# Another order for the same operations in a hand-scheduled kernel of linear attention, Fourier mixing and MLP

## The chip, the cores and the metric

The kernel runs on one core of a Trainium2 chip. The time is the device time of one execution in microseconds (us). A profile shows one execution; its span, from the first instruction to the last, is a little shorter than that execution's device time.

## What is computed

The inputs are r, k, v (4 batches, 8 heads, 768 steps, 48 dimensions), a decay w and a bonus u per head and dimension, and two weights of an MLP. The attention is a linear recurrence over the steps:

```python
for t in range(S):
    cur = einsum('bhd,bhe->bhde', u * k[t], v[t])
    y[t] = einsum('bhd,bhde->bhe', r[t], state + cur)
    state = w * state + einsum('bhd,bhe->bhde', k[t], v[t])
```

Its output x, 768 x 384 in each batch, goes through a Fourier mix and an MLP:

```python
u = x + real(fft(fft(x, axis=1), axis=2))
un = (u - mean(u)) / sqrt(var(u) + 1e-6)
out = u + relu(un @ w_ch1) @ w_ch2
```

## The kernel before

The work is cut into 24 chunks i of 128 steps, six in each batch b. The Python functions do not issue instructions at once. Each `op(...)` records an operation with a name, an engine, a planner's duration and a function that issues it; some have an alternative (`other=`) on another engine or in another form. The 1241 operations are numbered as they are recorded. At the end `sch.emit(_order(sch))` issues them as the string ORDER (lines 92 to 129) lists them: `543` issues operation 543 in its first form, `523.1` in its alternative. As each engine runs its own instructions strictly in this order, ORDER sets for every engine what stands behind what; the order within one engine is all that counts, and between engines semaphores take care. ORDER lists 1192 of the 1241 entries; those left out are some of the 90 idle fillers.

The names used below, with the lines of kernel.py:

- k i, r i, v i: loads of chunk i on the queue of SP (lines 279 to 290). The tiles kr and vt have 4 buffers each.
- KR i (302): VectorE scales k and r by powers of the decay. V i (310/311): a cast of v, on ScalarE or VectorE.
- tp i (316) and KRT i (325/326): transposes of KR on TensorE and their copy out of PSUM; from chunk 15 on KRT i is a transposing DMA on the SP queue (319).
- PR i (327), VectorE. A i (337): scores on TensorE, into two PSUM tiles.
- AC i,a with MA i,a: the causal mask of either half a. Either ScalarE copies the scores (344) and GpSimd masks the copy (346), or VectorE does both at once (349) and AC is nothing.
- u i (369/372) and S i+1 (381/383): the state's update on TensorE, and its copy, on VectorE or ScalarE.
- de i (401/406), DE i (412), TT i (414/417), y i (426): the output of chunk i; X i (435) adds TT on VectorE. In the other form an identity matmul, xt i (432), adds TT in PSUM, and ScalarE only copies X i (438). The PSUM tile yd_ps has one buffer, so de of the next chunk waits until X is done.
- EO, HH, XF (489, 495, 503/508 for batches 1 to 3, 455/469 for batch 0): the folds of the Fourier mix on VectorE, along steps and along dimensions. EO b,0,. takes chunks 0, 1, 3, 4 of batch b, EO b,2,. chunks 2 and 5.
- fp b,g,n (546), TT2 (555/558), TR (565/569), mp (586), xr (597), UF (599/605), UB (608/612): both Fourier products, the residual, the centred rows; st, MV, sd, rstd (617 to 655): the variance. st on ScalarE is line 619.
- UNT b,sh (661): the transpose of UB for the MLP, in batch 0 on TensorE (630), later a DMA on the SP queue.
- hp hf,ft (678): three matmuls of the MLP's first layer, for half batch hf = 2b+sh and a block ft of 12; HT hf,ft (683 on ScalarE, 686 on VectorE) is its ReLU. mo hf,j,half (698): six matmuls of the second layer; osb (705) adds, and out (709) stores on the SP queue.
- W1, W2 (735): weights, loaded on the GpSimd queue, each gated by a small copy (734) on a chunk's KR or V.
- idle (203): a matmul on zeros that does nothing but keep TensorE busy.

Nearly all short-lived PSUM results (hp, mo, fp, mp, tq, idle) share the ring "mm" of three buffers, so the fourth hp in a row waits until the first one's HT is done.

The order as it stands interleaves: chunks of batch b+1 are attended while the MLP of batch b fills TensorE. At the start TensorE has only chunks and fillers; at the end only the MLP of batches 2 and 3.

The operations that the text names have these numbers: xt12 470, X12 471, de14 502, DE14 503, xt15 523, y15 522, X15 524, AC16,1 530, AC16,0 532, u16 534, X16 541, EO2,0,1 543, KR17 550, V17 551, X17 564, KR18 571, A18 575, u18 580, KR21 622, KR23 664, KRT19 590, r23 207, fp1,0,0 767, fp1,1,0 771, UB1,0 788, st1,4 816, hp2,0 1013, HT2,0 1014, HT2,6 1030, HT2,7 1032, HT2,10 1042, HT2,11 1044, out1,1 1036, v15 184, k17 188, V0 213, KRT0 215, MA15,0 516.

Of the kernel before, what the change touches and what calls it, by code (L numbers as in the profile page):

```python
# [89 lines left out]


ORDER = """
95 93 135 90 110 91 101 137 117 102 108 116 118 109 114 94 129 96 111 138 92 136 132 0 97 104 140 1 112 98 2 103 99 3 105 119 4 113 115 5 120 106 141
6 107 121 139 7 124 8 212 123 9 142 125 214 122 143 100 10 144 215.1 11 12 13 230 126 217 146 127 213 14 15 133 218 232 134 147 216 220 222 131 219
233.1 224 231 16 149 225.1 17 221 223.1 130 235 226.1 18 128 150 234 238.1 228 227 252 240 19 20 145 21 236 229 254 241.1 239.1 237 148 242 22 255
243.1 244.1 23 24 152 274 246.1 245 257 247.1 209 256 276 258.1 260 248 264 249 277 153 25 292 26 27 28 265 151 253 259.1 261 294 275 262 278 279 295
263 266 29 280.1 30 281.1 155 284 282 268 267 250 285.1 297 251 154 269 31 283 211 298.1 32 286 210 296 33 314 287.1 34 300 685 692 156 693 293 699
288.1 301 316 299.1 157 290 289 948 317 700 302 291 686 160 270 304 303.1 318 319 305.1 306.1 949 158 315 706 707 322.1 323.1 320 308.1 307 271 309.1
273 272 324 310 694 321 708 325.1 326.1 687 701 311 328.1 327 159 312 329.1 313 702 330 695 161 331 709 710 332 688 333 689 947 711 690 696 697 691
712.1 703 704 698 35 705.1 713.1 334 715 162 721 716 335 722.1 717 727 723.1 344 163 336 728 729 718 36 724.1 37 719.1 730.1 735 737 337.1 739 736.1  # L100
720.1 738.1 740 339 338 353 953 714 340.1 342 345 164 741 954 346 343 753 742 743 725.1 747 165 950 754 755 744 969 748 726.1 749 167 756 761 970
750.1 765 168 762 745.1 763 766 975 764 731.1 746.1 370 977 976 732.1 1007 347 733.1 978.1 348 751.1 372 1008.1 973 373 752.1 341.1 350 1005 371.1 349
166 974 352 955 1006 979 757.1 169 956.1 354 388 980 362 758.1 959 170 363.1 971 734 355.1 960 963 172 972 356 390 964 406 171 357 391 957 358.1 359.1
173 989 360 392 965 389 990.1 361 175 375 958.1 966 380 951 376.1 378 174 1003 381 759.1 377.1 981 379 1004 176 1001 351 982 398 432 407 178 364 1002
967 399.1 760 374 393 952 968 416 396.1 394.1 397.1 434 365 417.1 995 395.1 366 435 983 996.1 368 367 991 984 369 177 437 433 436 992 382 440.1 438.1
441.1 408 179 383 384 961 409.1 993 962 439.1 386 385 994 985 410 455 387 411 454 986 412 180 414 413 456 987 182 415 400 457 464 1033 473.1 183 472
401 465.1 1034 181 458 402 474 1035 185 459 490 404 403 462.1 1045 460 186 475 405 461 188 482 463.1 418 997 508 419 988 491 998 476 184 483 420 477
999 187 422.1 421 480 525 492 190 423.1 1009 478 424 1036 425 442 500 493 1046 426 193 427 443 509 1000 494 1010 1047 444 196 501 495 428 446.1 1048
445 431 498.1 1021 526 1011 481 447.1 510 430 496 466 448 517 467 449 1022 518.1 451 1012 450 527 429 534 452 767 453 768 771 1023 468 769 772 189 773
770 499.1 775 776 479 191 470 774 469 777 779 471 497 780 778 781 484 782 572.1 512 192 535 485 785 511 515.1 513 791 783 1024 786 797 784.1 787 514  # L110
792.1 798 799 194 793.1 486 806 516.1 807.1 788 195 488.1 794.1 487 800 529 550 489.1 812 805 530.1 532.1 589 818 813 571 819.1 808.1 519 520 197
820.1 809.1 580 38 814 198 521 821 789 39 810.1 523 522 815.1 40 524 822.1 826 811.1 588 502 823.1 581.1 1013 528 199 503 533.1 1017 504 552 1014 1037
790 1018.1 816.1 506 1019 801 1038 1025 817.1 795 573 1020 597 605 1039 1026 598.1 505 1049 796 802 607 507 1040 1065 1050 606.1 536 551 1066.1 1015
803 200 531.1 537 614 824.1 1063 1016 804 553 554 201 825 615 538 1027 555 1064.1 1043 1028 540 574 539 203 1044 1053 556 541 1079 1054 542 204 559
557 543 1061 560 1080 206 608 1067 1062 544 1077 1068 545 207 1073 1078 622 1029 1074 202 1075 1030.1 561 1051 1076 590 1041 639 563 1052 575 1042
1031 546 205 578.1 576 547 1055 208 1032.1 558 1057 1056 664 623 562 624 1069 577 564 566 1058 565 579.1 549 1093 567 1059 609 568 1060 591 1094 610
548 570 612 569 582 1070 666 611 1095 583 625 592 584 1071 1096 827 828 593.1 595 594.1 829 1072 613 839 586 840 830 841 835 596 836 842 585 831 640
832 587 833 837 1081 834.1 838 667 843 844.1 845 1082 846 847 848.1 849.1 851 1083 616 852 631 850.1 853 617 1084 857 618 866 641 854 858 859 878 867
620 619 868 879 626 860 872 880 869 865 1117 873 874 627 861.1 875.1 1118 881.1 629 862.1 621 628 886 855.1 1105 870 630 1119 856.1 863.1 632.1 633
871 642 1106 1120 864 634 882 635 876 1085 1107 637 636 1091 1086 638 1108 668 877 1092 883 599 671.1 669 672.1 1121 600 884 648 601 643 1122.1 649.1  # L120
1089 885 644.1 603 646 602 1101 604 665 647 1115 1090 1102.1 670 650 645.1 1116 1145 651 1103 652 1146.1 1087 1104 654 653 1113 1088 655 1097 1114 656
673 1098 657 1109 674 1099 675 1110.1 1111 1100 658 677 1135 1112 659 676 1141 1136 678 680 1142 679 681 682 1129 660 662 663 661 1130 684 683 1143
887 888 1131 889 1144 891 892 890.1 893 1132 899 900 894 901 895 896 902 897 903 1125 898.1 1127 1126 904 905 1128 911 906 907 912.1 917 913.1 1147
918 919 908 1151 1148.1 914 926 920.1 1139 1152 927 928 925 938 1140 932 929 939 940 1153 933 934 941 1154 930.1 935.1 946 942.1 931.1 1133 1155 943.1
1137 1134 1156 1123 909.1 1138.1 1157 1124.1 915.1 910.1 1171 1158 1169 916.1 1172 1183 1170 1173 936.1 1184.1 1193 1174.1 921.1 937.1 1211 1194 1217
922.1 944.1 1212 1221 945 1218.1 923.1 1205 924 1222 1187 1206 1149 1188 1185 1150 1175 1186 1207 1176 1209 1208 1197 1210 1223 1198 1195 1224 1165
1196 1166 1199 1167 1159 1200 1168 1219 1160 1163 1220 1189 1164 1190 1177 1191 1192 1233 1178 1181 1179 1234 1182.1 1180 1237 1235 1236 1161 1229
1162 1238 1230 1239 1240 1213 1231 1232 1225 1201 1202 1214 1203 1204 1226 1215 1216 1227 1228
"""


# [652 lines left out]
```

## Time and profile before

| | |
|---|---|
| median of 13 runs | 185.38 us (182.84 to 189.43) |
| profiled execution | 184.95 us, span 183.2 us, mean granted TensorE clock 0.991 |
| TensorE busy | 164.9 us (90%), of it 12.4 us matmuls on zeros |
| VectorE busy | 141.1 us (77%) |
| ScalarE busy | 117.3 us (64%) |
| GpSimd busy | 44.2 us (24%) |
| HBM | 20.03 MB read, 4.72 MB written |

In the profile PE is TensorE, PEld its weight loads, DVE VectorE, ACT ScalarE, POOL GpSimd and SP the engine whose queue issues most DMAs (SPq). L302 is line 302 of the kernel. Busy time is the sum of instructions; matmuls overlap, and their ends are modelled. A row such as "L686 DVE ... x22 | 11.8, 550" means 22 instructions, 11.8 us in all, 550 ns each.

### The profile page before, as it was taken

Reading aid. Unit: us, or ns where it says so; the run is one execution under the profiler, and the core shown is the slowest. Engines: PE = TensorE matmul, PEld = TensorE weight load, DVE = VectorE, ACT = ScalarE, POOL = GpSimd, SP = SyncE. Lnnn points to the kernel's source line nnn. Section 1 sums busy time; section 2 is a strip of 40 time slices with the busy share of each in tenths; the row PEclk is TensorE's granted clock in tenths of the full one; section 3 lists DMA queues with packets and bytes.
Section 4 is the critical chain, followed back from the end, with each engine's and each line's share of the span. In section 5 each row is a group of like instructions: output and inputs, shape, how many; then the busy total and the mean of one; then the engine's idle time right before and its main releaser. Section 6 shows DMA issues by size and latency. Waiting matters only on the chain.

```text
span 183.2 us, 4289 instructions
## 1 busy us (share of the span) xinstructions
PE 164.9 (90%) x1624; PEld 107.6 (59%) x1626; DVE 141.1 (77%) x322; ACT 117.3 (64%) x277; POOL 44.2 (24%) x67
## 2 busy tenths in 40 slices
PE   4799878999998999769799899999999999999991
PEld 1256557666565666467456466876666765566650
DVE  7799698998998699978999999899698753014322
ACT  2888882999896346438988635796742899840100
POOL 5024352031362453403213215043410000000000
PEclk9999999999999999988999999999999999999999
DMA  4999999999999799999799895175002070011223
GB/s 99 206 189 201 236 233 205 194 183 203 208 175 221 147 204 254 211 178 198 127 228 200 169 210 148 47 165 155 0 0 84 14 163 2 4 43 55 74 86 129
DMA packets 97828, 26.79 MB, mean 146 GB/s; under 512 B 92432, under 2 KB 97168, under 8 KB 97808
## 3 DMA queue, kind: packets, MB, share of 16 engines
q1 hardware_dynamic: 94480, 23.77, 61.7%
q0 software_dynamic: 2144, 2.36, 8.1%
q10 hardware_dynamic: 1184, 0.39, 1.0%
q8 instruction: 12, 0.20, 0.4%
q14 instruction: 8, 0.07, 0.2%
HBM read 20.03 MB, written 4.72 MB: 135 GB/s over the span
## 4 chain that ended last, share of the span: by engine, by line
PE 47%; DVE 29%; DMA 14%; issue 5%; SPq 2%; ACT 1%; DVEq 0%
PE mm L678 17%; PE mm L698 15%; DMA kr<-in_r_dram 8%; DVE KR L302 6%; PE mm L546 4%; PE mm L586 3%; DMA kr<-in_k_dram 3%; DMA UNT<-UB 2%; DVE X L435 2%; DVE PR L327 2%; DVE EO L489 2%; PE A_ps L337 2%; DVE HH L495 2%; DVE UF L599 2%; DVE MA L349 2%
## 5 line engine op out<-in xcount | busy, mean ns | idle before, releaser
L678 PE MATMUL mm<-UNT,W 128*128 128x384 bf16 x288 | 53.3, 326 | 1.3 <-DVE HT L686 0.9
L698 PE MATMUL mm<-W,HT 128*128 128x384 bf16 x288 | 50.7, 326 | 1.0 <-DMA W<-in_moe_w_ch_dram 1.0
L683 ACT ACTIVATE HT<-mm 128x384 bf16<-128x384 f32 x74 | 35.4, 490 | 16.8 <-PE mm L678 16.5
L698 PEld LDWEIGHTS <-HT 128*128 128x128 bf16 x288 | 27.1, 98 | 17.9 <-DMA W<-in_moe_w_ch_dram 1.4
L678 PEld LDWEIGHTS <-W 128*128 128x128 bf16 x288 | 26.4, 97 | 17.2 <-issue 1.8
L705 DVE SCALAR_TENSOR_TENSOR osb<-mm,rstd,UF 128x384 f32<-128x384 f32 x24 | 14.6, 611 | 22.4 <-PE mm L698 22.4
L346 POOL TENSOR_SCALAR_AFFINE_SELECT MA<-AC 128x512 bf16<-128x512 bf16 x27 | 19.1, 714 | 52.2 <-ACT AC L344 51.4
L414 POOL TENSOR_TENSOR TT<-V,DE 128x384 bf16<-128x384 bf16 x19 | 17.0, 897 | 33.6 <-ACT DE L412 27.8
L302 DVE TENSOR_TENSOR KR<-kr,wtab 128x768 bf16<-128x768 f32 x24 | 22.9, 956 | 2.1 <-DMA kr<-in_r_dram 1.7
L344 ACT CAST AC<-A_ps 128x512 bf16<-128x512 f32 x27 | 15.5, 585 | 8.9 <-PE A_ps L337 8.7
L546 PE MATMUL mm<-te_t,XF 128*128 128x193 bf16 x99 | 12.3, 257 | 3.2 <-DVE XF L503 2.1
L203 PE MATMUL mm<-zero 128*128 128x512 bf16 x39 | 12.4, 426 | 2.8 <-DVE zero L219 2.7
L349 DVE TENSOR_TENSOR MA<-A_ps,mtri 128x512 bf16<-128x512 f32 x21 | 14.2, 680 | 0.0
L686 DVE TENSOR_SCALAR HT<-mm 128x384 bf16<-128x384 f32 x22 | 11.8, 550 | 2.6 <-PE mm L678 2.5
L555 ACT CAST TT<-mm 97x386 bf16<-97x386 f32 x11 | 6.1, 597 | 11.7 <-PE mm L546 11.7
L310 ACT CAST V<-vt 128x384 bf16<-128x384 f32 x20 | 10.2, 512 | 4.7 <-DMA vt<-in_v_dram 3.2
L546 PEld LDWEIGHTS <-XF 128*128 128x128 bf16 x120 | 10.0, 101 | 5.0 <-DVE XF L503 2.2
L327 DVE TENSOR_TENSOR PR<-KRT 128x512 bf16<-128x512 bf16 x24 | 12.3, 514 | 0.1
L435 DVE TENSOR_TENSOR X<-yd_ps,TT 128x384 bf16<-128x384 f32 x18 | 9.9, 552 | 3.2 <-PE yd_ps L426 3.1
L325 ACT COPY KRT<-tp 128x1024 bf16<-128x1024 bf16 x10 | 10.1, 1014 | 2.6 <-PE tp L316 2.5
L599 DVE SCALAR_TENSOR_TENSOR UF<-mm,X 128x384 f32<-128x384 f32 x19 | 10.2, 556 | 1.8 <-PE mm L586 1.5
L619 ACT ACTIVATE lw<-UF,sm 128x384 f32<-128x384 f32 x18 | 11.0, 613 | 0.6 <-DVE UF L599 0.4
(90 smaller groups left out, 230.4 us busy)
## 6 DMA issues: line engine op xcount, KB each, us to landing
kr<-in_k_dram SPq DMA_DIRECT2D x24, 192.0 KB, 4.1
vt<-in_v_dram SPq DMA_DIRECT2D x24, 192.0 KB, 4.1
out_dram<-osb SPq DMA_DIRECT2D x24, 192.0 KB, 1.9
kr<-in_r_dram SPq DMA_DIRECT2D x23, 192.0 KB, 3.9
W<-in_moe_w_ch_dram POOLq DMA_DIRECT2D x6, 384.0 KB, 6.7
te_t<-te_c SPq DMA_DIRECT2D x1, 579.0 KB, 5.3
hid_t<-hid_c SPq DMA_DIRECT2D x1, 288.0 KB, 3.9
wrow<-in_w_dram ACTq DMA_DIRECT2D x1, 192.0 KB, 3.8
```

The costliest lines, as they stand in the source:

```text
L302: op(("KR", i), "DVE", 960, lambda: nc.vector.tensor_tensor(out=KR().rearrange("t s p (a d) -> t (s p) a d", a=2)[:, :, :, 0:D], in0=kr(). ...
L327: op(("PR", i), "DVE", 410, lambda: nc.vector.tensor_tensor(out=PR(), in0=KRT()[:, 0], in1=KRT()[:, 1], op=AluOp.mult), r=[("KRT", i)], w= ...
L344: op(("AC", i, a), "ACT", 590, lambda: nc.scalar.copy(AC(), A_ps[a]()), r=[("A", i)], w=[("AC", i, a)], new=[AC], use=[A_ps[a]], pri=pri, ...
L346: op(("MA", i, a), "POOL", 630, lambda: nc.gpsimd.affine_select(out=MA[a](), in_=AC(), pattern=[[0, NP], [1, 128]], base=0, channel_multip ...
L349: port=True, other=[("DVE", 680, False, lambda: nc.vector.tensor_tensor(out=MA[a](), in0=A_ps[a](), in1=mtri.unsqueeze(1).to_broadcast([12 ...
L414: op(("TT", i), "POOL", 830, lambda: nc.gpsimd.tensor_tensor(out=TT(), in0=V(), in1=DE().unsqueeze(2).to_broadcast([128, H, D]), op=AluOp. ...
L546: nc.tensor.matmul(fp()[:, par, :], lhsT=lhsT[:, g * CH:g * CH + 128], rhs=rhs, start=(nb == 0 and par == 0), stop=(nb == last and par == ...
L599: op(("UF", b, blk), "DVE", 650, lambda: nc.vector.scalar_tensor_tensor(out=parity(UF()[:, j, :]), in0=mp(), scalar=1.0, in1=parity(X()[:, ...
L678: nc.tensor.matmul(hp(), lhsT=W1[:, dt, ft * 128:(ft + 1) * 128], rhs=UNT()[:, :, dt, :], start=(dt == 0), stop=(dt == 2))
L683: op(("HT", hf, ft), "ACT", 495, lambda: nc.scalar.activation(out=HT()[:, ft, :], in_=hp(), func=Act.Relu, scale=-1.0), r=[("hp", hf, ft)] ...
L698: nc.tensor.matmul(mo(), lhsT=HT()[:, ft, j * 128:(j + 1) * 128], rhs=W2[:, ft, :], start=(ft == 0), stop=(ft == 11))
L705: op(("osb", hf, j), "DVE", 620, lambda: nc.vector.scalar_tensor_tensor(out=osb(), in0=mo(), scalar=rstd()[:, j:j + 1], in1=UF()[:, j, :], ...
```

## The change

Only the string ORDER differs. No operation, tile, wait or duration is edited. 1192 entries stand in either string. What changes is the place of many entries and the form of about 120. By kind, before and after: HT on ScalarE 74 and 81, on VectorE 22 and 15; masks on GpSimd 27 and 26, on VectorE 21 and 22; X on VectorE 18 and 16, on ScalarE 6 and 8, with as many xt matmuls (6 and 8); KRT on ScalarE 10 and 8, on VectorE 5 and 7; S on ScalarE 13 and 12, on VectorE 7 and 8. The number of idle fillers is the same.

The lines of ORDER that hold the operations named above, before (-) and after (+):

```diff
-95 93 135 90 110 91 101 137 117 102 108 116 118 109 114 94 129 96 111 138 92 136 132 0 97 104 140 1 112 98 2 103 99 3 105 119 4 113 115 5 120 106 141
-6 107 121 139 7 124 8 212 123 9 142 125 214 122 143 100 10 144 215.1 11 12 13 230 126 217 146 127 213 14 15 133 218 232 134 147 216 220 222 131 219
+118 93 135 90 108 114 110 91 137 101 117 109 95 116 111 94 102 92 98 138 136 105 0 97 129 1 107 140 96 2 112 3 132 99 113 104 4 119 5 106 120 141 6
+103 121 7 139 115 122 8 212 9 124 143 10 123 214 125 142 100 11 144 215 12 13 230 14 15 146 126 217 134 127 131 213.1 232 216 218 147 222 133 224 220
...
-401 465.1 1034 181 458 402 474 1035 185 459 490 404 403 462.1 1045 460 186 475 405 461 188 482 463.1 418 997 508 419 988 491 998 476 184 483 420 477
-999 187 422.1 421 480 525 492 190 423.1 1009 478 424 1036 425 442 500 493 1046 426 193 427 443 509 1000 494 1010 1047 444 196 501 495 428 446.1 1048
-445 431 498.1 1021 526 1011 481 447.1 510 430 496 466 448 517 467 449 1022 518.1 451 1012 450 527 429 534 452 767 453 768 771 1023 468 769 772 189 773
-770 499.1 775 776 479 191 470 774 469 777 779 471 497 780 778 781 484 782 572.1 512 192 535 485 785 511 515.1 513 791 783 1024 786 797 784.1 787 514
-792.1 798 799 194 793.1 486 806 516.1 807.1 788 195 488.1 794.1 487 800 529 550 489.1 812 805 530.1 532.1 589 818 813 571 819.1 808.1 519 520 197
-820.1 809.1 580 38 814 198 521 821 789 39 810.1 523 522 815.1 40 524 822.1 826 811.1 588 502 823.1 581.1 1013 528 199 503 533.1 1017 504 552 1014 1037
-790 1018.1 816.1 506 1019 801 1038 1025 817.1 795 573 1020 597 605 1039 1026 598.1 505 1049 796 802 607 507 1040 1065 1050 606.1 536 551 1066.1 1015
-803 200 531.1 537 614 824.1 1063 1016 804 553 554 201 825 615 538 1027 555 1064.1 1043 1028 540 574 539 203 1044 1053 556 541 1079 1054 542 204 559
-557 543 1061 560 1080 206 608 1067 1062 544 1077 1068 545 207 1073 1078 622 1029 1074 202 1075 1030.1 561 1051 1076 590 1041 639 563 1052 575 1042
-1031 546 205 578.1 576 547 1055 208 1032.1 558 1057 1056 664 623 562 624 1069 577 564 566 1058 565 579.1 549 1093 567 1059 609 568 1060 591 1094 610
+455 459 1035 402 474 185 460.1 462 997 473.1 404 475 458 186 403 998 463 405 1036 508 418 184 492 419 491 999 420 464 1045 188 461.1 465.1 476 988
+422.1 421 525 477 423.1 187 482 442 424 483.1 1009 425 1000 443 493 426 190 500 1046 427 478 193 480 428 1010 444 1047 510 431 446.1 445 501 1021 509
+479 1011 1048 447.1 526 196 494 517 449 466 495 448 467 430 1022 451 498.1 496 1012 450 518.1 429 527 453 771 452 767 768 1023 468 769 772 773 770
+499.1 534 189 775 497 470.1 774 469 191 776 572.1 777 471.1 779 783 780 778 781 511 484 192 782 512 481 535 485 785 513 486 515.1 516.1 194 791 784.1
+786 797 787 514 792.1 1024 488.1 798 799 487 793.1 529 788.1 806 800 195 794.1 807.1 818 489.1 550 819.1 808.1 805 519 812 571 820.1 37 813 520 810.1
+814 197 521 580 38 198 532 789 811.1 523.1 809.1 815 522 39 821.1 524.1 588 826 530 502 40 551 581 533 503 816.1 1013 801 199 1037 528 552 817.1 1014
+790 504 802 1017 795 1038 1015 822.1 1018.1 506 505 796 573 1039 589 531 823.1 507 1016 1019 605 1040 536 1020 1049 200 824.1 1065 803 1050 606.1 597
+607 825 804 1077 1066 598 537 1025 1078 1067 553 1026 201 538 1053 1068 614 554 1054 203 540 615 1027 555.1 557 556.1 539 1043 1028 574 204 1063 558
+1044.1 575 541 1064 206 1029 578 542 1061 576 590 608 559 543 1030 1041 560 1062 609 561 1042.1 207 1031 610 202 544 563 1079 1032 622 1073 1080 1055
+1074 205 545 1075 1056 546 1069 547 208 1076 639 562 624 1057 564 579 664 612 1070 623 565 592 611 1071 1051 548 1072 582 1058 566 1052 641 549 583
```

## The prediction

> **What bounds the kernel now.** I read first the slices of the page, to see which engine is full when (each digit is 4.58 us).
>
> ```profile
> PE   4799878999998999769799899999999999999991
> DVE  7799698998998699978999999899698753014322
> PEclk9999999999999999988999999999999999999999
> DMA  4999999999999799999799895175002070011223
> ```
>
> There are three stages. Up to about 65 us the DMA row is at 9: input chunks arrive no faster, and TensorE fills its waits with matmuls on zeros (39, 12.4 us in all). From 65 to 105 us VectorE is nearly full and TensorE has holes. From there to the end TensorE is at 9 without a break. The granted clock dips once, in the middle stage. The busy times by stretch (length, then PE, PEld, DVE, ACT, POOL, clock, DMA share, GB/s) size this:
>
> ```profile
> 72.00:78.00 6.00, 4.73 (x50) 2.74 (x47) 5.97 (x12) 2.53 (x7) 3.31 (x5) 1.00 1.19 223
> 78.00:84.00 6.00, 4.74 (x52) 4.04 (x53) 4.42 (x12) 2.77 (x6) 0.00 (x0) 0.74 0.99 196
> 84.00:90.00 6.00, 4.92 (x64) 3.64 (x63) 5.73 (x15) 5.64 (x17) 2.43 (x3) 0.98 0.74 141
> 90.00:96.00 6.00, 5.28 (x53) 3.41 (x53) 5.66 (x14) 5.27 (x16) 0.83 (x1) 1.00 1.08 213
> 96.00:102.00 6.00, 6.00 (x60) 3.77 (x58) 5.97 (x13) 5.24 (x15) 2.98 (x4) 1.00 1.05 201
> 102.00:108.00 6.00, 5.13 (x45) 2.95 (x43) 5.58 (x10) 3.40 (x8) 0.74 (x2) 1.00 0.89 173
> 150.00:160.00 10.00, 10.00 (x62) 5.93 (x61) 2.04 (x6) 9.46 (x24) 0.00 (x0) 1.00 0.08 25
> ```
>
> TensorE idles 1.27+1.26+1.08+0.72+0.87 = 5.2 us here. After 108 us it idles some 0.2 us up to its end at 179.5. So a wait removed in the middle stage shortens the run, and one that is added lengthens it. Which waits they are, the timeline of TensorE tells (start, duration; in brackets the idle time before and who ended it):
>
> ```profile
> 76.52 0.26 PE L546 MATMUL mm<-te_t,XF 128*128 128x193 bf16 x1
> 78.86 0.34 PE L546 MATMUL mm<-te_t,XF 128*128 128x193 bf16 x2 [2.09 <-DVE XF L503]
> 79.61 1.28 PE L546 MATMUL mm<-te_t,XF 128*128 128x193 bf16 x13 [0.40 <-DVE XF L508]
> ...
> 88.25 0.34 PE L369 MATMUL u_ps<-V,KR 128*128 128x96 bf16 x4 [0.48 <-DVE KR L302]
> 90.31 0.24 PE L401 MATMUL yd_ps<-UW,PR 128*128 128x2 bf16 x4 [0.87 <-DVE X L435]
> 104.37 0.65 PE L678 MATMUL mm<-UNT,W 128*128 128x384 bf16 x3 [0.87 <-DVE HT L686]
> ```
>
> The first pair is fp1, the Fourier matmuls of batch 1, behind the fold EO, HH, XF on VectorE. Then u18 waits for KR18. At 90.31 de14 waits for X15, as yd_ps has one buffer. At 104.37 an mlp1 matmul waits for HT2.6, which VectorE runs behind KR21 (102.90, 0.94 us). Right after the first pair the clock falls:
>
> ```profile
> 80.80:84.30 3.50, 3.50 (x40) 3.00 (x39) 2.09 (x6) 2.51 (x7) 0.12 (x1) 0.51 1.10 238
> ```
>
> **What the Trainium skill says.** "TensorE: Matmul & The Clock Gate", part 1 (The HAM clock gate), says that TensorE falls to half clock after an idle window of about 3.4 us and recovers after a busy one, and that the windows run free of the kernel. The trace agrees on rate and length (0.51 for 3.5 us), though TensorE was not wholly idle: 1.91 of 4.40 us busy from 76.4 to 80.8. "SBUF — State Buffer", section "SBUF: two separate sides", says that VectorE and GpSimd share a port pair as an exclusive lock, so that an operation of either blocks the other for its whole length. The trace agrees: the two wide HH of batch 1 took 2.11 us from 71.36 on, with a GpSimd TT (71.33) and a mask (72.11) beside them; those of batch 3, with GpSimd idle, 1.10. "Perfetto Trace Analysis", section "Tensor Engine Instruction", calls ACT, DVE and GPSIMD strict FIFO: what waits holds all behind it, as HT2.6 shows.
>
> **The change, part by part.** No operation is added except two identity matmuls (xt12, xt15), because X12 and X15 move from VectorE to ScalarE. All else is order and choice of engine.
>
> *Start to fp1.* KRT0 moves to ScalarE behind the six table exponentials (end 8.84): 8.84+1.01 = 9.85, against 8.45+0.69 = 9.14 before; V0 goes to VectorE. The chain then waits for chunk 5's load to 22.83 anyway, so I take 0. Without that cover it costs 0.7. On SP, v12 and v13 move behind r14, which lets KR13 and KR14 come earlier and V12, V13 later; out1.1 moves ahead of v15 and k17, whose data are wanted 17 us later. The bytes ahead of chunk 16 are the same, and KR16 started at 69.45, about 4 us (median landing 3.9) after its r was issued at 65.39. So EO1 begins at the same time: 0, within -0.5 to +0.7. The two weight loads that swap places on the POOL queue have the same bytes and gates: 0, inside the same bounds.
>
> *fp1.* The same operations stand between KR16 and the last XF, so the wait ends at the same time. u16 (0.28 us, 76.23 to 76.52) was done before the wait and now stands behind it: +0.28. xt12 is one more matmul there: +0.17 (start to start of the like one at 68.65). fp1.1.0 goes in front and takes two matmuls out: -0.17. Sum +0.28, at half clock up to +0.6; at least 0.
>
> *KR18 and u18.* VectorE does MA15.0 (0.68) before UF1.0, where it idled, and no longer between; UB1.0 (0.41) comes in. KR18 ends 0.27 earlier; I take -0.2 of u18's wait of 0.48, bounds -0.48 and 0.
>
> *X15 and HT2.0.* On ScalarE stand from about 88.0, UF1.5 being done: st1.3 0.80, AC16.0 0.59, UB1.4 0.61, X15 0.48, end 90.5. Before, X15 ended on VectorE at 89.71+0.55 = 90.26. Then AC16.1 0.59, V17 0.51, DE14 0.17, st1.4 0.80, HT2.0 0.49: end 93.0, against 91.49+0.49 = 92.0. The PSUM ring mm has three buffers, so the fourth mlp1 group waits for HT2.0. Counting on from 93.0 with 0.49 a group, y14 0.20 and de16 0.27, eight groups are done at 95.92 with u19 (0.17) still owed; before, eight and u19 at 95.86. So +0.23, taken as +0.3; bounds -0.3 (X15 runs before UB1.4's inputs matter) and +1.1 (one AC and V row, 0.59+0.51, more in front).
>
> *HT2.6 and HT2.7* go to ScalarE; VectorE gets HT2.11 and HT2.10 instead, behind X16 and EO2.0.1, none behind a KR. The wait of 0.87 goes: -0.87. Next late would be ScalarE: A18's two AC rows (1.17) stand before HT2.6, and counting as above each group finds its buffer with 0 to 0.2 us to spare. Bounds -0.87 and 0. On SP, KRT19 (1.3 us of issue) moves ahead of r23; KR23 now runs behind X17, which waited for y17 until 107.7, past r23's landing near 105.5+1.3: 0, uncovered +1.3.
>
> *From 105 us* TensorE is full with the same work; the last osb and its DMA (3.7 us after the last matmul) are the same. VectorE loses HTs there (22 to 15 over the run), which only adds slack: 0.
>
> Sum: 0+0.28-0.2+0.3-0.87 = -0.49. The profiled execution took 184.95 (span 183.2 and 1.75 around): 184.46. The median of the 13 runs is 0.43 above it: 185.38-0.49 = 184.89, say **184.9**.
>
> **Rivals.**
>
> *The clock stays up* (183.2). TensorE was busy for all 3.50 us at 0.51, so the dip cost at most 3.5x(1-0.51) = 1.7. If the two matmuls of fp1.1.0 within the wait, or the four scattered fillers before hp2.0 where three stood close together, keep a window busy enough, it goes: 184.9-1.7 = 183.2. For: spread of the runs, 182.84 to 189.43, shows that something that large comes and goes. Against: the wait itself stays.
>
> *ScalarE becomes the bound, slower.* Between the first TT2 of batch 1 and of batch 2 it gains two HT (0.98), two X (0.96), two AC (1.17) and loses two S (1.28) and a UB (0.61): +1.2 us, where from 84 to 102 it idles 0.36+0.73+0.76 = 1.85. If HT2.0 ends later than about 94, and HT2.6 behind A18's copies, each makes TensorE wait for a row of copies, 1.1 and 0.9: 184.9+2.0 = 186.9. For: strict order and three mm buffers. Against: the sum still fits.
>
> *Nothing gained, nothing lost*: the 0.87 comes back as the port lock, since two more masks (0.64 each) run on GpSimd in this stage beside VectorE's folds: 184.9+0.87, about 185.8. It lies within the forecast's own band.
>
> **How the numbers follow.** About 0.5% (0.9 us) is what a measurement of this kernel can tell from no change, so no change is 184.45 to 186.3. The forecast with the third rival (184.0 to 186.0) has 0.38: 0.08 under 184.45, 0.27 within, 0.03 above. The clock rival has 0.33, all faster but 0.02. The ScalarE rival has 0.29, slower but for 0.01. Faster 0.39, same 0.30, slower 0.31. The range leaves out a tenth at either side: 182.5 (clock rival less the -0.5 of the start, rounded) to 187.4 (ScalarE rival with the start's +0.5); the likeliest case's own range is 184.0 to 186.0.
>
> **What would show it.** HT before mlp1's first wait near 104 is no longer named, and TensorE is full from about 102; X15 ends near 90.5 and HT2.0 near 93.0, both on ScalarE; XF still ends a wait of about 2 us in fp1. It is wrong if fp1 starts more than 0.7 us earlier or later, if TensorE shows holes after 108 us, or if the clock row differs.

## The result

| comparison | kernel | median of it, us | median of the kernel before, us | ratio, 95% interval |
|---|---|---|---|---|
| first | changed | 183.70 (11 runs) | 185.70 | 0.9905 [0.9866, 0.9943] |
| second, chip 1 | changed | 180.81 (6) | 184.87 | 0.9783 [0.974, 0.9827] |
| third, chip 12 | changed | 181.20 (6) | 184.01 | 0.9825 [0.9771, 0.9878] |
| second, chip 1 | before, once more | 185.29 (22) | 184.87 | 1.0015 [0.9976, 1.0054] |

The ratios and their intervals leave out executions that took more than 1.5% longer than the fastest of their kernel, while the medians count all, so the two need not agree.

The change makes the kernel faster by 1 to 2%. The forecast had the side right (184.9, likeliest case -0.49 us), but the medians differ by 2.0 us in the first comparison and by 4.1 and 2.8 us in the two repeats, four to eight times the sum. The first median lies within the predicted range (182.5 to 187.4 us), those of the repeats lie below it.

The profile taken with the first comparison is of its longest execution (185.91 us). In it KR16 started at 70.58 us, later than in either profile of the kernel before, and hp2.0 waited for the transpose UNT1.0, whose DMA took 6.15 us from issue to landing:

```profile
91.88 2.33 PE L678 MATMUL mm<-UNT,W 128*128 128x384 bf16 x8 [2.03 <-DMA UNT<-UB]
```

So the changed kernel is shown below from the third comparison (180.80 us, span 179.0; UNT1.0 took 3.49 us), against the repeat of the kernel before (184.43 us, span 182.6). Both have a granted clock of 1.00 throughout, so the clock takes no part in the difference of these two.

The slices of the changed kernel, 4.48 us each:

```profile
PE   4789896989999899969889999999999999999991
DVE  7699999899999899989997999996796953231412
PEclk9999999999999999999999999999999999999999
DMA  4999999999999989998999895193002250020223
```

TensorE is at 9 from slice 22 on, where the kernel before reached it at slice 24. VectorE's row is fuller in the first third. The stretches, in the same columns as above (length, then PE, PEld, DVE, ACT, POOL, clock, DMA share, GB/s):

```profile
72.00:78.00 6.00, 3.94 (x44) 2.27 (x42) 5.93 (x14) 2.17 (x6) 2.44 (x3) 1.00 1.12 179
78.00:84.00 6.00, 6.00 (x94) 5.29 (x92) 5.46 (x15) 5.34 (x13) 1.42 (x2) 1.00 1.04 216
84.00:90.00 6.00, 5.15 (x60) 3.18 (x59) 6.00 (x14) 5.96 (x20) 2.93 (x4) 1.00 0.86 150
90.00:96.00 6.00, 5.48 (x56) 3.42 (x54) 4.48 (x12) 5.44 (x14) 1.06 (x1) 1.00 1.10 214
96.00:102.00 6.00, 6.00 (x63) 3.54 (x61) 5.97 (x11) 5.05 (x13) 3.32 (x4) 1.00 0.94 179
102.00:108.00 6.00, 6.00 (x54) 3.60 (x53) 5.93 (x14) 2.81 (x7) 1.38 (x2) 1.00 0.97 205
```

TensorE idles 2.06+0.85+0.52 = 3.43 us here; the repeat of the kernel before idles 5.32. The waits on TensorE's timeline (in brackets the idle time and its releaser):

```profile
77.79 1.11 PE L546 MATMUL mm<-te_t,XF 128*128 128x193 bf16 x11 [1.83 <-DVE XF L508]
85.32 0.34 PE L369 MATMUL u_ps<-V,KR 128*128 128x96 bf16 x4 [0.38 <-DVE KR L302]
87.09 0.24 PE L401 MATMUL yd_ps<-UW,PR 128*128 128x2 bf16 x4 [0.35 <-ACT X L438]
90.89 0.65 PE L678 MATMUL mm<-UNT,W 128*128 128x384 bf16 x3 [0.52 <-DVE HT L686]
```

XF still ends the wait in fp1. de14 waits 0.35 instead of 0.79 us, for ScalarE's X15. The wait near 104 us is gone, and a smaller one for VectorE's HT2.2 has come at 90.89. After it TensorE has no wait of 0.15 us or more.

The repeat of the kernel before has these at the same places:

```profile
79.03 0.34 PE L546 MATMUL mm<-te_t,XF 128*128 128x193 bf16 x2 [2.09 <-DVE XF L503]
79.78 1.28 PE L546 MATMUL mm<-te_t,XF 128*128 128x193 bf16 x13 [0.41 <-DVE XF L508]
...
89.41 0.24 PE L401 MATMUL yd_ps<-UW,PR 128*128 128x2 bf16 x4 [0.79 <-DVE X L435]
...
103.68 0.65 PE L678 MATMUL mm<-UNT,W 128*128 128x384 bf16 x3 [0.90 <-DVE HT L686]
```

So the difference of the two spans, -3.6 us, divides by milestones (us from the span's start):

| stretch | before | after | difference | predicted |
|---|---|---|---|---|
| start to KR16's start | 69.47 | 67.80 | -1.67 | 0 |
| to the end of the last XF of batch 1 | 79.72 | 78.13 | +0.08 | 0 |
| to the end of fp1 | 81.94 | 80.45 | +0.10 | +0.28 |
| to the start of hp2.0 | 90.01 | 87.57 | -0.95 | -0.2+0.3 |
| to the start of fp2 | 112.59 | 109.17 | -0.98 | -0.87 |
| to the end | 182.6 | 179.0 | -0.18 | 0 |

The table is of one pair, and its rows are not equally firm. Every kernel tried below but three (those that move loads) runs one of the two orders unchanged up to KR16, so their profiles add to the first row. Leaving out three in which a dip of the clock came before it, KR16 started at 69.45, 69.47, 69.04 and 68.32 us in the order before and at 70.58, 67.80, 67.82 and 69.23 in the changed one. These overlap, so a gain at the start is not shown; -1.67 is what this pair has. From KR16's start to the end the executions agree: 113.1 us in the kernel before and 113.2 in it with the ten matmuls on zeros, both without a dip, against 111.2 in both repeats of the changed kernel. These 1.9 us are the firm part; in the first comparison's profile the wait for UNT1.0 and a dip of the clock took them back (113.6).

Two rows missed in this pair: the start and the stretch from fp1 to hp2.0. The experiments test them, the HT row and the clock.

### The profile page after: what moved, and what is told of

Its sections match the earlier page's. It is cut to its first block, busy times and chain, and to the rows that moved or that the text cites. A ratio compares the mean times of both kernels' runs of the same rounds, so it can differ in the third digit from the quotient of the medians.

```text
span 184.2 us, 4299 instructions
## 1 busy us (share of the span) xinstructions
PE 165.6 (90%) x1627; PEld 107.6 (58%) x1628; DVE 141.6 (77%) x320; ACT 117.8 (64%) x278; POOL 46.9 (25%) x66
## 4 chain that ended last, share of the span: by engine, by line
PE 42%; DVE 28%; DMA 13%; ACT 7%; issue 5%; SPq 4%; DVEq 0%; ACTq 0%
PE mm L678 17%; PE mm L698 16%; DMA kr<-in_r_dram 8%; DVE KR L302 4%; PE mm L546 3%; DMA UNT<-UB 3%; DVE MA L349 3%; DVE PR L327 3%; DMA vt<-in_v_dram 2%; PE mm L586 2%; DVE HH L495 2%; DVE EO L489 2%; DVE X L435 2%; DVE XF L508 2%; SPq L283 1%
## 5 line engine op out<-in xcount | busy, mean ns | idle before, releaser
L678 PE MATMUL mm<-UNT,W 128*128 128x384 bf16 x288 | 54.3, 333 | 2.3 <-DMA UNT<-UB 2.0
L683 ACT ACTIVATE HT<-mm 128x384 bf16<-128x384 f32 x81 | 38.6, 489 | 15.8 <-PE mm L678 15.4
L414 POOL TENSOR_TENSOR TT<-V,DE 128x384 bf16<-128x384 bf16 x19 | 20.2, 1062 | 50.2 <-ACT DE L412 47.0
L302 DVE TENSOR_TENSOR KR<-kr,wtab 128x768 bf16<-128x768 f32 x24 | 23.8, 999 | 4.4 <-DMA kr<-in_r_dram 4.2
L203 PE MATMUL mm<-zero 128*128 128x512 bf16 x40 | 13.1, 445 | 2.6 <-DVE zero L219 2.5
L546 PE MATMUL mm<-te_t,XF 128*128 128x193 bf16 x99 | 11.5, 248 | 2.3 <-DVE XF L508 1.2
L686 DVE TENSOR_SCALAR HT<-mm 128x384 bf16<-128x384 f32 x15 | 7.9, 550 | 5.2 <-PE mm L678 5.2
L327 DVE TENSOR_TENSOR PR<-KRT 128x512 bf16<-128x512 bf16 x24 | 11.6, 490 | 0.0
L337 PE MATMUL A_ps<-KRT 64*128 64x128 bf16 x192 | 10.0, 219 | 1.7 <-DVE MA L349 1.0
L435 DVE TENSOR_TENSOR X<-yd_ps,TT 128x384 bf16<-128x384 f32 x16 | 8.8, 550 | 3.4 <-PE yd_ps L426 3.4
```

What stands on the lines that cost most here:

```text
L203: op("idle", "PE", 216, lambda: nc.tensor.matmul(z(), lhsT=zero[:, 0:128], rhs=zero, start=True, stop=True), r=["zero"], w=[("idle", len(s ...
L302: op(("KR", i), "DVE", 960, lambda: nc.vector.tensor_tensor(out=KR().rearrange("t s p (a d) -> t (s p) a d", a=2)[:, :, :, 0:D], in0=kr(). ...
L327: op(("PR", i), "DVE", 410, lambda: nc.vector.tensor_tensor(out=PR(), in0=KRT()[:, 0], in1=KRT()[:, 1], op=AluOp.mult), r=[("KRT", i)], w= ...
L414: op(("TT", i), "POOL", 830, lambda: nc.gpsimd.tensor_tensor(out=TT(), in0=V(), in1=DE().unsqueeze(2).to_broadcast([128, H, D]), op=AluOp. ...
L546: nc.tensor.matmul(fp()[:, par, :], lhsT=lhsT[:, g * CH:g * CH + 128], rhs=rhs, start=(nb == 0 and par == 0), stop=(nb == last and par == ...
L678: nc.tensor.matmul(hp(), lhsT=W1[:, dt, ft * 128:(ft + 1) * 128], rhs=UNT()[:, :, dt, :], start=(dt == 0), stop=(dt == 2))
```

## The experiments

Each ratio is to the kernel before, measured on the same chip. Entries in a diff are those of ORDER, "..." marks what lies between.

### Both kernels once more

The first four kernels were to part two causes, waits that leave TensorE's path and the clock, and to show how far the comparison repeats.

> The kernel before, unchanged, for a second profile and the granted clock of several runs. Theory A (waits removed, the 0.87 us behind HT2.6 above all): a clock dip of one window in the middle, as in the first profile, in about as many runs as with the changed kernel. Theory B (the clock): the dip in most runs of this kernel (0.991 or so) and in few of the changed one. Ratio to the kernel before 1.00.

> The changed kernel, unchanged, for a profile that is not disturbed. Theory A: span about 181.5; no wait for UNT of 2 us as in the first profile, no dip of the clock or one as often as before, TensorE full from about 102 us. Theory B: no dip in most runs. Ratio to the kernel before 0.990.

The results are in the first table. The repeat of the changed kernel gained more than I expected. Its profiled execution had one window of half clock early on (30.2 to 33.6 us), which put KR6 at 34.52 instead of 32.89 us, and still took 182.21 us.

### The HT swap alone, in either direction

The kernel before with the engines of four HT exchanged:

```diff
-1044 ... 1030.1 ... 1042 ... 1032.1
+1044.1 ... 1030 ... 1042.1 ... 1032
```

> The kernel before with one part of the change alone: HT2.6 and HT2.7 on ScalarE, HT2.10 and HT2.11 on VectorE, places kept. Theory A: the wait of 0.87 us near 104 is gone and the run shorter by it, ratio 0.995. Theory B: ratio 1.00, the dip as before. If VectorE's new HTs make TensorE wait as long, 1.00 too, with the wait named there.

Measured: 0.9925 [0.9882, 0.9967], but the medians of all executions are closer (184.56 and 184.87 us, a ratio of 0.998), so the size of the gain is uncertain. In its profiled execution the wait near 104 us is gone, but hp3 waits for the transpose UNT1.1, and a de waits for the X ahead of it:

```profile
97.71 1.15 PE L678 MATMUL mm<-UNT,W 128*128 128x384 bf16 x6 [0.53 <-DMA UNT<-UB]
...
103.20 0.24 PE L401 MATMUL yd_ps<-UW,PR 128*128 128x2 bf16 x4 [0.28 <-DVE X L435]
```

From hp2.0 to fp2 it needed 22.58 us, as much as the kernel before: in the old order the next waits took back what the swap freed. The reverse, in the changed kernel, with KR21 put ahead of HT2.7:

```diff
-1044.1 ... 1030 ... 1042.1 ... 1032 622
+1044 ... 1030.1 ... 1042 ... 622 1032.1
```

> The changed kernel with HT2.6 and HT2.7 back on VectorE behind KR21, as before, and HT2.10 and HT2.11 on ScalarE. If the swap gains its 0.87 us in this order too (it gained 0.75% in the kernel before): a wait of 0.6 to 0.9 us for HT returns between 102 and 105 us, ratio 0.982 to 0.983. Rival: in the new order VectorE reaches KR21 earlier and the wait does not return: 0.978 +- 0.0015.

Measured: 0.9821 [0.9773, 0.9868] (the changed kernel: 0.978 and 0.9825 on other chips; the intervals overlap). The profile is sharper than the ratio. HT2.6 stays ahead of KR21 here, unlike in the kernel before, so it is HT2.7, behind KR21, that TensorE waits for:

```profile
101.77 1.14 PE L678 MATMUL mm<-UNT,W 128*128 128x384 bf16 x6 [1.03 <-DVE HT L686]
```

From hp2.0 to fp2 it needed 22.31 us, against 21.60 in both repeats with the swap and 22.58 before the change. The swap is thus worth 0.7 us in the new order.

### X on VectorE or on ScalarE

The changed kernel with X12 and X15 on VectorE, without xt12 and xt15:

```diff
-470.1 471.1 523.1 524.1
+470 471 523 524
```

> The changed kernel with X12 and X15 back on VectorE and without their two identity matmuls. My prediction priced X15 on ScalarE at +0.3 us. If that holds, this is 0.1 to 0.3 us faster than the changed kernel: ratio about 0.976 where the repeat had 0.978. Theory A, from the trace of the repeat, where de14's wait fell from 0.79 to 0.35 and hp2.0 began 0.9 us earlier: the move of X to ScalarE is what gains, and taking it back costs 0.4 to 0.9 us: 0.980 to 0.983. Rival: other parts of the order (UB1.0, UB1.5 and V19 that left ScalarE) gain it, and X may run on either: 0.978 +- 0.001. In the profile de14's wait tells: 0.35 or 0.8.

Measured: 0.9851 [0.9801, 0.9902], 182.05 us; the interval overlaps those of the changed kernel. In the profile X15 ended at 87.98 instead of 87.04 us and hp2.0 began at 88.52 instead of 87.57, but KR16 had started 0.59 us later too. Counted from KR16's start, X15 ended after 19.59 us, against 19.24 in the changed kernel and 18.53 and 18.43 in it with HT or the loads back; hp2.0 began after 20.13 us, against 19.77, 19.68 and 19.50. TensorE's timeline of this kernel:

```profile
88.04 0.24 PE L401 MATMUL yd_ps<-UW,PR 128*128 128x2 bf16 x4 [1.30 <-DVE X L435]
```

The same two on ScalarE in the kernel before:

```diff
-470 471 523 524
+470.1 471.1 523.1 524.1
```

> The kernel before with X12 and X15 on ScalarE, by an identity matmul each. If X on ScalarE gains by itself: de14's wait falls from 0.8 to 0.35, hp2.0 begins about 0.4 us earlier, ratio 0.995 to 0.998. If it needs the lighter row of ScalarE that the new order has (UB1.0, UB1.5 and V19 elsewhere): X15 ends later than on VectorE, HT2.0 is 0.5 us late, ratio 1.000 to 1.005. My prediction's term of +0.3 us is a ratio of 1.0016.

Measured: 0.9996 [0.996, 1.0032], 184.87 us. Here de14's wait fell to 0.35 us, but hp3 then waited 0.42 for the transpose UNT1.1:

```profile
89.83 0.24 PE L401 MATMUL yd_ps<-UW,PR 128*128 128x2 bf16 x4 [0.35 <-ACT X L438]
93.97 1.15 PE L678 MATMUL mm<-UNT,W 128*128 128x384 bf16 x6 [0.42 <-DMA UNT<-UB]
```

From fp1's end to hp2.0 the new order needs 8.36 us with X back, and with X on ScalarE 7.12 (both repeats), 7.73 (HT back) and 7.66 (loads back). In the last two, as with X back, the fold of batch 1 ended sooner behind KR16 (see the last section), de14 ran 1.1 us sooner than with X back, counted from KR16, and then hp2.0 waited 0.45 and 0.37 us for UNT1.0. The old order needs 8.07 us, 7.73 with the ten matmuls on zeros, and 7.70 with X on ScalarE. So at hp2.0 the move is worth 0.4 to 0.6 us in the new order, counted from KR16, and nothing that can be measured in the old one. The traces point to ScalarE's row ahead of it for the difference; no kernel tried moved that row alone. ScalarE in the changed kernel:

```profile
84.27 0.53 ACT L605 ACTIVATE UF<-mm 128x384 f32<-128x384 f32 x1
...
84.79 0.65 ACT L619 ACTIVATE lw<-UF,sm 128x384 f32<-128x384 f32 x1
...
85.40 0.61 ACT L344 CAST AC<-A_ps 128x512 bf16<-128x512 f32 x1
85.87 0.66 ACT L608 ACTIVATE UB<-UF,sm 128x384 bf16<-128x384 f32 x1
86.56 0.48 ACT L438 CAST X<-yd_ps 128x384 bf16<-128x384 f32 x1
...
88.49 0.88 ACT L683 ACTIVATE HT<-mm 128x384 bf16<-128x384 f32 x2
```

and in the repeat of the kernel before (UB1.0 and UB1.2 in one line, V19, UF1.5, UB1.5):

```profile
84.56 1.12 ACT L608 ACTIVATE UB<-UF,sm 128x384 bf16<-128x384 f32 x2
...
85.95 0.52 ACT L310 CAST V<-vt 128x384 bf16<-128x384 f32 x1
...
87.18 0.53 ACT L605 ACTIVATE UF<-mm 128x384 f32<-128x384 f32 x1
...
87.81 0.62 ACT L608 ACTIVATE UB<-UF,sm 128x384 bf16<-128x384 f32 x1
```

It is the row that I had listed (st1.3, AC16.0, UB1.4, X15), but it starts at 84.8, not at 88.0: UF1.5, with the reading of its sum, is done 4.42 us after fp1's end, against 5.84 in the kernel before, where UB1.0 and V19 stood ahead of it on ScalarE and UB1.5 right behind it.

### The loads alone, taken back, and with the HT swap

The kernel before with the changed order of its loads from chunk 12 on (v12 175, v13 178, r14 180, out1.1 1036, v15 184):

```diff
-175 ... 178 ... 179 ... 180 ... 188 ... 184 ... 1036
+179 180 175 178 ... 1036 184 188
```

> The kernel before with only its loads in the changed order from chunk 12 on: v12 and v13 behind r14, out1.1 and v15 ahead of k17. My prediction priced this at 0. Theory A: the load order gains the 1.1 to 2.2 us by which the fold of batch 1 ends earlier in the changed kernel (osb no longer waits 0.34 us for out1.1 at 75.7, KR13 and KR14 come earlier): ratio 0.990 to 0.995. Rival B: VectorE's own order and the place of GpSimd's masks gain it (0.6 us less from KR16 to the last XF), loads nothing: 0.999 +- 0.002. Rival C: V12 and V13 stand where they stood on ScalarE and VectorE, now wait for their loads, and hold what is behind them: 1.002 to 1.008.

Measured: 1.0176 [1.012, 1.0231], 187.14 us. Rival C holds, and costs more than I allowed. r16 landed at 67.03 us (69.17 and 68.01 in two executions of the old order), but KR16 began at 70.65. ScalarE's V12 waits for the load that is now behind r14 (first line), and VectorE's V13 likewise, with KR13 behind it:

```profile
61.10 0.51 ACT L310 CAST V<-vt 128x384 bf16<-128x384 f32 x1 [3.92 <-DMA vt<-in_v_dram]
```

```profile
62.93 0.68 DVE L311 CAST V<-vt 128x384 bf16<-128x384 f32 x1 [2.62 <-DMA vt<-in_v_dram]
63.53 0.94 DVE L302 TENSOR_TENSOR KR<-kr,wtab 128x768 bf16<-128x768 f32 x1
```

In the changed kernel V13 stands behind KR14, and V12 too is further back on its engine. Taken back in the changed kernel:

```diff
-174 ... 177 ... 175 178 ... 1036 184 188 988 ... 190
+175 174 ... 178 177 ... 188 988 184 ... 190 1036
```

> The changed kernel with v12 and v13 ahead of r12 and r13 again, and out1.1 behind v17, v15 behind out0.0, as before. Theory A: 0.5 to 1% of the gain goes, 0.984 to 0.990 beside about 0.979 for the changed kernel of the same call. Rival B: same as the changed kernel to 0.2%. In the profile, KR13, KR14 and KR16 tell, and whether osb waits for an out DMA.

Measured: 0.9827 [0.9748, 0.9905], too wide to tell from the changed kernel's 0.9825 on the same chip. In its profile VectorE waits for r13 and r14:

```profile
61.58 0.96 DVE L302 TENSOR_TENSOR KR<-kr,wtab 128x768 bf16<-128x768 f32 x1 [0.60 <-DMA kr<-in_r_dram]
64.06 0.96 DVE L302 TENSOR_TENSOR KR<-kr,wtab 128x768 bf16<-128x768 f32 x1 [1.52 <-DMA kr<-in_r_dram]
```

KR16 began at 69.19 us, 1.39 later than in the changed kernel, but fp1 ended only 0.58 later (81.03), since in this execution GpSimd's work held up the fold of batch 1 less (see the last section). But 69.19 lies among the starts of the changed order itself (67.80 to 70.58), and in the one with 70.58 VectorE had waited for loads of r too, 0.98 and 0.62 us. So what the new load order gains is shown neither by the ratio nor by this profile.

The load order with the HT swap, in the kernel before:

```diff
-1044 ... 1030.1 ... 1042 ... 1032.1
+1044.1 ... 1030 ... 1042.1 ... 1032
```

> The kernel before with the load order of the run with loads alone and with HT2.6, HT2.7 on ScalarE and HT2.10, HT2.11 on VectorE. If the two parts add: 0.9925 (the HT swap alone) times the ratio of the loads alone, 0.983 to 0.988 under theory A, 0.992 under rival B.

Measured: 1.0127 [1.0076, 1.0179], which overlaps the loads alone. TensorE's wait for HT2.6 is gone, but hp3 waits 0.44 us for UNT1.1, and from hp2.0 to fp2 the gain is 0.2 us (22.48 against 22.69).

### Matmuls on zeros in the wait for XF

Ten in the kernel before and eight in the changed one, ahead of fp1.0.0:

```diff
+                if b == 1 and g == 0 and nb == 0:
+                    for _ in range(10):
+                        nc.tensor.matmul(fp().rearrange("c a m -> c (a m)"), lhsT=zero[:, 0:128], rhs=zero[:, 0:386],
+                                         start=True, stop=True, skip_group_check=True)
```

> The kernel before with ten matmuls on zeros (386 columns, 1.6 us in all) ahead of fp1.0.0, inside the wait of 2.09 us for XF. Theory B: the dip of the clock after fp1 is gone in most runs, ratio 0.991 to 0.994. Theory A: the dip is not what the change removed; ratio 1.00, or below if the dip costs both kernels the same. If the fillers delay fp1, up to 1.005.

Measured: 0.9918 [0.9886, 0.995], 183.82 us. The wait shrank to 0.59 us (the lines of this kernel are 4 higher):

```profile
76.14 1.80 PE L542 MATMUL mm<-zero 128*128 128x386 bf16 x10
...
78.61 0.34 PE L550 MATMUL mm<-te_t,XF 128*128 128x193 bf16 x2 [0.59 <-DVE XF L503]
```

> The changed kernel, with eight matmuls on zeros (386 columns each) put ahead of fp1.0.0, inside the wait for XF. The kernel before gained 0.8% from ten of them, and its clock then fell in few executions. Theory A (the order's gain is waits alone; the clock is a second, separate cost): the changed kernel loses the clock in fewer executions already, so fillers are worth at most 0.3% more than the 0.978 of its repeat: 0.975 to 0.98. Theory B (the changed kernel still pays for the dip as often as the kernel before): 0.97 to 0.974. Theory C (fillers delay fp1, as XF ends about when they do): 0.98 to 0.985. In the profile the wait for XF shrinks from about 1.8 us to under 0.6 and the clock row shows no 5 or 8 between 76 and 90 us.

Measured: 0.9859 [0.9802, 0.9915], 182.38 us: no gain over the changed kernel. Theory C, and by my own placing: fp1.1.0 stands ahead of fp1.0.0 in the new order and waits for the last XF, so the zeros ran behind the wait. fp1 ended 3.32 us after the last XF, not 2.32. (In this execution KR16 was late as well, at 69.23.)

```profile
78.14 0.26 PE L550 MATMUL mm<-te_t,XF 128*128 128x193 bf16 x1 [1.24 <-DVE XF L508]
78.23 1.47 PE L542 MATMUL mm<-zero 128*128 128x386 bf16 x8
79.54 1.02 PE L550 MATMUL mm<-te_t,XF 128*128 128x193 bf16 x10
```

### The changed kernel a third time

> The changed kernel, unchanged, a third comparison with the kernel before. The first comparison gave 0.9905, the repeat 0.978, and kernels that share its order up to 100 us gave 0.982 to 0.986. If the repeat is the rule: 0.975 to 0.982, last XF of batch 1 at 77.0 to 78.0 us in an execution without a dip, TensorE full from 93 us on. If the first comparison is the rule: 0.987 to 0.993.

Measured: 0.9825 [0.9771, 0.9878]; its profile is the one shown above. It is nearer to the second comparison than to the first, whose interval it overlaps too. Why the first showed only 0.9905 is not settled; its one profile has the late KR16 and the wait for UNT1.0 shown above. The clock alone is not the reason: nine of its executions had no dip of the clock, and yet a median of 183.56 us, against 180.77 of five such in the second.

## Why the prediction was right or wrong

The side was right and the sum too small. The terms for fp1 and for HT held in kind; those for the start, for u18 and for X15 each had a wrong step, so that the first median lies within the range says little for the whole.

*Start to fp1, taken as 0: the reason was wrong, the size is open (-1.67 us in this pair).* By the prediction's own sign, fp1 starting more than 0.7 us earlier, the step fails here: 75.70 us against 76.68. The step is "the bytes ahead of chunk 16 are the same ... So EO1 begins at the same time". The bytes are the same, and yet r16 landed at 67.31 us instead of 69.17, with KR16 0.3 to 0.5 us behind it in either. I counted bytes on the queue and not the waits of VectorE, whose row also ends at KR16: KR16 runs right behind PR13 or osb0.1. VectorE's waits from 20 us to KR16 sum to 0.96+0.37+0.23+1.13+0.20+1.31 = 4.20 us in the repeat of the kernel before and to 0.36+0.23+0.23+0.68+0.35 = 1.85 in the changed one. The longest of either, before and after:

```profile
45.64 0.96 DVE L302 TENSOR_TENSOR KR<-kr,wtab 128x768 bf16<-128x768 f32 x1 [1.13 <-DMA kr<-in_r_dram]
...
61.23 0.62 DVE L705 SCALAR_TENSOR_TENSOR osb<-mm,rstd,UF 128x384 f32<-128x384 f32 x1 [1.31 <-PE mm L698]
```

```profile
60.21 0.62 DVE L705 SCALAR_TENSOR_TENSOR osb<-mm,rstd,UF 128x384 f32<-128x384 f32 x1 [0.68 <-PE mm L698]
```

But the new order does not fix these waits. In the changed kernel with eight zeros, which stand behind KR16, the same wait was 1.70 us, as TensorE itself waited 1.60 us for the last piece of W2 to land (0.58 in the third comparison, 0.53 in the repeat of the kernel before); its lines are 4 higher:

```profile
61.43 0.62 DVE L709 SCALAR_TENSOR_TENSOR osb<-mm,rstd,UF 128x384 f32<-128x384 f32 x1 [1.70 <-PE mm L702]
```

There the sum was 3.09 us and KR16 started at 69.23; in the first comparison it was 3.90 us and KR16 stood at 70.58. Shown is that equal bytes do not make equal starts, and that the new load order without the new places of V12 and V13 delays KR16 (70.65, and 72.29 with the HT swap, against 68.32 to 69.47). Whether the new order as a whole gains the start, and whether loads or VectorE then set it, stays open.

*fp1, +0.28: right in kind, +0.10.* "The wait ends at the same time" held for its length (KR16 to the last XF 10.25 and 10.33 us).

*KR18 and u18, -0.2: wrong.* The wait is 0.38 us in every profile of the changed kernel, against 0.48 and 0.28 in the two of the kernel before. KR18 did end 0.55 us earlier behind fp1 (4.81 us after it, not 5.36), but TensorE reached u18 earlier too, which the term left out.

*X15 and HT2.0, +0.3: wrong, with the sign.* The mis-sized term is the start of ScalarE's row, 88.0, taken from when UF1.5 was done in the old order; it started at 84.8. My own list of ScalarE's gains and losses had a UB going out, but I used the old time. From the start of the row on, the sum was good: 2.5 us to X15's end against 2.25 measured, and 2.5 to HT2.0's end against 1.95. The stretch gained 0.95 us in the pair where -0.2+0.3 was predicted; taking X back cost 0.4 to 0.6 us of it.

*HT2.6 and HT2.7, -0.87: right in the new order.* The stretch gained 0.98 us in the pair, and reversing the swap lost 0.7; the bounds were -0.87 and 0. In the old order the traces show 0 and 0.2 us. The next late one was not ScalarE's HT2.6, as I had it, but VectorE's HT2.2 at 90.89, 0.52 us.

*From 105 us and on SP, 0: right.* -0.18 from fp2 to the end, no wait of 0.15 us or more.

*The rival "the clock stays up": in part.* Its 183.2 is the number nearest to the first median, 183.70, but that is luck, as the pair above gains 3.6 us without the clock. A window of 3.4 us at half speed lowers the mean granted clock by about 3.4 x 0.5/182 = 0.009, wherever it lies. The mean is below 0.9945 in 75 of 105 executions of the kernel before (beside the experiments, its repeat among them), and in 6 of 24 of the changed one. In the second comparison the former took 185.32 us in the median with it and 184.12 without, 1.2 us and not the bound of 1.7. An estimate from these is that fewer dips add about (0.71-0.25) x 1.2 = 0.55 us to what the pair shows. That a fuller wait keeps the clock is shown in the kernel before: with ten matmuls on zeros 2 of 16 executions were below, without them 35 of 53 on the same chip. "TensorE: Matmul & The Clock Gate", part 1, of the Trainium skill speaks of an idle window. Here a dip followed 4.4 us in which TensorE was busy 43% of the time in the first profile of the kernel before, and none followed the same waits in its repeat. What decides was not found.

*The rival "ScalarE becomes the bound": no.* HT2.0 ended at 88.99, before my 93.0, and no wait for ScalarE's HT appeared. *The rival "nothing gained": no.* The port lock did not give the 0.87 back: in the changed kernel KR21 grew from 0.94 to 1.38 us, which no TensorE wait followed.

No kernel tried was faster than the changed one beyond its interval.

## What to carry to other kernels

When an order changes, price each wait with the row of the new order and not with the times at which the old one reached it: an operation that is moved to an engine starts when what was taken off that engine is gone. Equal bytes ahead of a load do not make its stage equal: one and the same order reached KR16 at 67.80 and at 70.58 us here, so look at several executions before a gain at such a place is priced or explained. Move loads and their consumers together: the loads alone cost 1.8%, about as much as the whole change gains. A swap that frees a wait should be followed to the next wait in line, which took back all or most of it in the order before.

## What the runs showed of the hardware

The port lock makes the same fold, in the same order, take different times. In two executions whose VectorE and GpSimd reach the fold of batch 1 at the same time to 0.03 us, GpSimd's TT12 won the port in one (DVE and then GpSimd of the changed kernel):

```profile
74.65 0.99 DVE L503 TENSOR_TENSOR XF<-HH 128x392 bf16<-128x392 bf16 x1
75.56 1.49 DVE L495 TENSOR_TENSOR HH<-EO 128x384 bf16<-128x384 bf16 x2
```

```profile
74.39 1.02 POOL L414 TENSOR_TENSOR TT<-V,DE 128x384 bf16<-128x384 bf16 x1 [2.55 <-ACT DE L412]
```

and VectorE in the other (the changed kernel with HT back):

```profile
74.68 0.35 DVE L503 TENSOR_TENSOR XF<-HH 128x392 bf16<-128x392 bf16 x1
74.95 0.62 DVE L495 TENSOR_TENSOR HH<-EO 128x384 bf16<-128x384 bf16 x2
```

```profile
74.42 2.12 POOL L414 TENSOR_TENSOR TT<-V,DE 128x384 bf16<-128x384 bf16 x1 [2.54 <-ACT DE L412]
```

The last XF ended at 78.13 and 77.47 us: 0.66 us from one decision of the lock, with TT12 taking 1.02 or 2.12 us. That agrees with the exclusive lock that "SBUF — State Buffer", section "SBUF: two separate sides", of the Trainium skill describes (on VectorE's side for operations in a two-port mode or with two inputs in SBUF, as these folds have), and adds that who wins is not fixed by the order: in both executions VectorE's second EO had started 9 ns ahead of TT12. Here the 0.66 us did not reach the MLP. hp2.0 began at 87.57 and 87.50 us, because after the faster fold it waited 0.45 us for UNT1.0, whose DMA took 4.55 us instead of 3.49.
